# Where 16 output sums of a two-attention kernel are kept until they are stored

## The chip, the cores and the metric

The kernel runs on one core of one Trainium2 chip. The metric is device time in microseconds of one execution, lower is better; several executions give a median. A profile of one execution gives the time of each instruction on the core's engines: TensorE (PE, matrix products), VectorE (DVE), ScalarE (ACT), GpSimd (POOL) and SyncE (SP), and of the DMA transfers that SP, ACT and POOL issue. Each engine works through its own instructions in order and waits on semaphores where it needs another's result. In the profile's notation `ost<-g,r` is an instruction that reads the tiles g and r and writes ost.

## The reference, cut to what matters

Two attention layers on separate inputs, both of 2048 rows and 1024 columns with 32 heads, their outputs side by side:

```python
def _A_ref(x, wqkv, wo):      # each row looks at 8 rows, two apart
    qkv = (x @ wqkv) ...
    logits = einsum("bhsd,bhswd->bhsw", q, kg) * scale   # masked
    o = einsum("bhsw,bhswd->bhsd", softmax(logits), vg)
    return o @ wo
def _B_ref(x, wqkv, wo):      # each row looks at the 256 rows up to its own
    ...
    return o @ wo
return concatenate([_A_ref(...), _B_ref(...)], axis=-1)
```

All data is float32. The part that matters here is the last product of layer A, `o @ wo`.

## The kernel before

Work is cut into eight units of 512 rows: units 0 to 3 are layer B (dense), units 4 to 7 layer A (window). Each unit has eight groups of four heads; group s of unit u has the number hg = 8u + s, so the last is 63. A planner written in Python (`Clock`) simulates the engines with fixed durations and writes the instructions of all engines out in one order; what an engine does next is settled when the program is made, not while it runs. The semaphores between the engines are put in by the framework from what each instruction reads and writes.

A float32 product is made as three products of parts: `Stream.parts` splits a raw tile into a high part (a cast, L276 on ScalarE or L279 on VectorE) and a low part (the difference, L282 on VectorE), and each 128-row step of a product takes three matmuls (`mm`, L324, which is every matmul's line). Raw tiles are loaded by POOL's queue (L221) as tiles come free.

For layer A the outputs of two units are multiplied with `wo` together, in seven products instead of eight of half the size (`product(u, i)` for u = 4 and 6, i = 0 to 6). Products 0 and the like take tiles as they are; the others take sums of quarters, made earlier by VectorE (L1133) and kept in DRAM (`sd`, `td`), while the windows' outputs are kept in `od`. Each product has four column blocks n of four steps, so 12 matmuls per block; a block is summed in one of three PSUM banks ("g") and then added by VectorE (`add`, L902) to what the earlier products gave. These 14 products come at the end of the program, one after the other; the last steps of the last windows (groups 62 and 63: scores, mask L1214, softmax, values "o") lie between the first of them.

In products 1 and 4 an output block is complete. There are four blocks in each, so for two pairs of units 16 in all, counted by `where_o["ot"]`. Each is written by `add` to a tile o and stored from it by ScalarE's queue (L908). `going` holds stores that are not yet issued: a new sum first issues the older ones. Before the change, o was one of two things:

- the tile "ost" of the pool `stp`, which has a single buffer (`NST = 1`), so that each new sum there waits until the store of the one before has landed;
- columns 1024 to 1536 of `band[b]`, the working tile of the windows' softmax for even or odd groups, when group 62 + b is finished (`done["o"]`) and the count is not a multiple of three.

The seats are two stretches of the tile `pbuf`, one for even and one for odd groups, of 2 x 512 + 8 columns: the layer-A rows of queries (first 512) and keys (the rest) that the scores of a window read. In the profile they have the name pbuf. SP copies them there from the "nat" tiles (L608); `seat_free` notes in `done["scores"]` that the scores of a group have been issued. The last window's scores are those of hg = U * NG - 1 = 63.

Of the kernel before, what the change touches and what calls it, by code (L numbers as in the profile page):

```python
# [7 lines left out]
F32 = mybir.dt.float32  # L8
# [6 lines left out]
P = 128  # L15
NG = 8
NK = 8
S = 512
# [273 lines left out]
def kernel(ctx, tc, xs, wqk, wv, wo, outs, units):  # L292
# [3 lines left out]
    U = len(units)  # L296
# [10 lines left out]
    stp = ctx.enter_context(tc.tile_pool(name="stp", bufs=NST))  # L307
# [11 lines left out]
    def mm(out, left, right, **k):  # L319
        issued[0] += 4 if left.dtype == F32 else 2  # L320
        n = int(issued[0] + EXTRA - ASKED) // CHUNK
        if n > asked[0]:
            asked[:] = n, ck.now
        nc.tensor.matmul(out, left, right, **k)  # L324
# [30 lines left out]
    done = {}  # L355
# [102 lines left out]
    where_o = {"ot": 0, "s": 0, "bg": 0}  # L458

    def slot(i):  # L460
        return roomp.tile([P, 1024], F32, tag=f"r{i % NO}", name="r")
# [65 lines left out]
    seats = more[:, :2 * (2 * S + 8)].rearrange("p (b c) -> p b c", b=2)  # L527
    band, wide = [None, None], [None, None]
    halo = [[dram.tile([P, 2, 256], F32, name=f"halo{i}_{s}") for s in range(NG)] for i in range(2)]

    xt, xready, ot, rows, waiting = {}, {}, {}, {}, {}
# [32 lines left out]
    def latest(*ts):  # L564
        return None if any(t is None for t in ts) else max(ts)
# [288 lines left out]
    def product(u, i):  # L854

        out = []
        h = totals.setdefault(u, {})

        def ready(n, k):
            if n == 0 and k == 0:  # L860
                for j in range(2):
                    if ("s", u, i, j) not in held:
                        at = where["p", u, i, "s", j]
                        st.split_to(at + 1)
                        if at not in st.ready:
                            return None
                        held["s", u, i, j] = st.get(at)
            if n % 2 == 0 and k == 0 and ("t", u, i, n // 2) not in held:
                at = where["p", u, i, "t", n // 2]
                st.split_to(at + 1)  # L870
                if at not in st.ready:
                    return None
                held["t", u, i, n // 2] = st.get(at)
            x, r = held["s", u, i, k // 2]
            r = max(r[k % 2], held["t", u, i, n // 2][1])
            return latest(rg.when(), r) if k == 0 else r

        def run(n, k):
            if k == 0:
                h["ps"], h["b"] = rg.take()  # L880
            w, x = held["t", u, i, n // 2][0], held["s", u, i, k // 2][0][k % 2]
            c = S * (n % 2) + P * k
            for t, (a, b) in enumerate(TERMS):
                mm(h["ps"], w[:, a, c:c + P], x[:, b, :], start=(k == 0 and t == 0),
                                 stop=(k == 3 and t == 2))
            if k == 1:
                at = where["p", u, i, "t", 1]
                more_w = [kind for kind, _ in st.items[at + 1:at + 1 + (n + 1 if n else 0)]]
                while more_w.count("w") > 1 + n // 2:
                    more_w.pop()  # L890
                st.split_to(at + 1 + len(more_w))

        def after(n, k):
            if k < 3:
                return
            ps, bank = h["ps"], h["b"]
            if i == 0 and n % 2 == 0:
                h["ac", n // 2] = [slot(8 + 2 * g + n // 2) for g in range(2)]
            a, c = [t[:, S * (n % 2):S * (n % 2) + S] for t in h["ac", n // 2]]

            def add(dst, src):
                nc.vector.tensor_tensor(dst, ps, src, op=ALU.add)  # L902
                return ck.use("dve", 0.61, ck.now + ck.SEM)

            def store(r, col, tile, e):
                def go():
                    if going.pop(key, None):
                        nc.scalar.dma_start(outs[ORDER[u + r], 4 * col + n], tile)  # L908
                        ck.load("store", e)

                key = u, r, col, n
                going[key] = go
                ck.defer(e, go)

            if i in (1, 4):
                for f in list(going.values())[:-1]:
                    f()
                where_o["ot"] += 1
                b = where_o["ot"] % 2
                o = band[b][:, 1024:1536] if where_o["ot"] % 3 and U * NG - 2 + b in done["o"] else stp.tile([P, S], F32, tag="ost", name="ost")  # L920
            if i == 0:
                nc.scalar.copy(a, ps)
                e = ck.use("act", 0.485, ck.now + ck.SEM)
            elif i == 1:
                e = add(o, a)
                store(0, 0, o, e)
            elif i == 2:
                e = add(a, a)
            elif i == 3:
                e = add(c, a)  # L930
            elif i == 4:
                e = add(o, c)
                store(1, 0, o, e)
            elif i == 5:
                e = add(c, c)
                store(1, 1, c, e)
                e = add(a, a)
            else:
                e = add(a, a)
                store(0, 1, a, e)  # L940
            rg.give(bank, e)

        for n in range(4):
            for k in range(4):
                at = (n, k)
                out.append((lambda at=at: ready(*at), lambda at=at: run(*at), 3 * CG, lambda at=at: after(*at)))
        return out
# [611 lines left out]
    for u in range(U):  # L1559
        for s in range(NG):  # L1560
            a, b = attention(u, s)
# [58 lines left out]
    while True:  # L1620
# [21 lines left out]
        t, name = best  # L1642
# [54 lines left out]
```

## Time and profile before

| | |
|---|---|
| runs | 1792.06, 1794.24, 1795.07 us; median 1794.24 |
| the profiled execution | 1793.36 us |
| its span (first to last instruction) | 1791.7 us |
| mean granted clock of TensorE | 0.998 |
| busy: PE, VectorE, ScalarE, GpSimd | 1771.8, 1295.5, 936.3, 412.2 us |
| first and last sum at L902 | 1640.2 and 1787.6 us after the span's start |

Times in the profile's views are counted from the span's start. A row of a timeline has start, length, engine, line, operation, what is written and read, the count of merged instructions, and in brackets the engine's idle time just before with what ended it.

### The profile page before, as it was taken

What the parts mean: (1) busy time and instruction counts of PE and PEld (TensorE: products, weight loads), DVE (VectorE), ACT (ScalarE), POOL (GpSimd) and SP (SyncE); (2) the same over time, 40 slices, a digit from 0 to 9 for tenths busy, and PEclk for the clock granted to TensorE, in tenths of its full rate; (3) what the DMA queues carried; (4) which work ended last, traced back from release to release, by engine and by line L of the source; (5) the groups of instructions that cost most, each with busy time, mean ns of one, the idle gap of its engine ahead of it and who ended that gap; (6) DMA issues with size and microseconds to landing.
All of it is one profiled execution on the core that took longest, in us unless ns stands there. A gap on an engine that the chain in (4) does not pass through costs nothing.

```text
span 1791.7 us, 38433 instructions
## 1 busy us (share of the span) xinstructions
PE 1771.8 (99%) x14496; PEld 1443.6 (81%) x14496; DVE 1295.5 (72%) x2881; ACT 936.3 (52%) x2332; POOL 412.2 (23%) x962
## 2 busy tenths in 40 slices
PE   9999999999999999999999999999999999999999
PEld 7787777888778888878788788888888887887887
DVE  6777876768867769867678556566577869677966
ACT  5565566555656565656554524533354455455442
POOL 3322323222342223332223410100011101001210
PEclk9999999999999999999999999999999999999999
DMA  8355664644656556555556266666576769848984
GB/s 258 105 149 136 186 168 136 170 136 142 186 141 165 151 134 166 154 146 146 147 136 185 61 189 190 199 201 202 171 232 207 213 181 290 291 139 274 303 318 143
DMA packets 154793, 324.57 MB, mean 181 GB/s; under 512 B 18032, under 2 KB 58992, under 8 KB 154608
## 3 DMA queue, kind: packets, MB, share of 16 engines
q0 software_dynamic: 45792, 166.74, 30.9%
q1 hardware_dynamic: 98736, 137.02, 26.9%
q10 hardware_dynamic: 10080, 18.35, 2.8%
q8 instruction: 115, 1.88, 0.5%
q14 instruction: 70, 0.57, 0.1%
HBM read 201.33 MB, written 53.48 MB: 142 GB/s over the span
## 4 chain that ended last, share of the span: by engine, by line
PE 94%; DMA 2%; DVE 1%; ACT 1%; issue 1%; SPq 0%; DVEq 0%; ACTq 0%; POOLq 0%
PE g L324 74%; PE s L324 13%; PE o L324 7%; DMA outs<-ost 0%; DMA raw<-sd 0%; ACT s L1400 0%; DMA pbuf<-nat 0%; DVE w L282 0%; DMA raw<-wqk 0%; DMA raw<-xs 0%; DMA qst<-nat 0%; ACT w L276 0%; DVE r L1133 0%; DVE qst L1435 0%; DVE x L282 0%
## 5 line engine op out<-in xcount | busy, mean ns | idle before, releaser
L324 PE MATMUL g<-x,w 128*128 128x512 f32 x3552 | 879.1, 394 | 5.3 <-DVE ost L902 3.5
L324 PEld LDWEIGHTS g<-x,w 128*128 128x128 f32 x3552 | 658.6, 189 | 135.2 <-issue 10.7
L282 DVE TENSOR_TENSOR w<-raw,w 128x512 fp32r<-128x512 f32 x510 | 334.4, 697 | 53.7 <-ACT w L276 47.5
L1395 DVE CUSTOM_DVE_ANT_0 s<-s,mask_d 128x384 f32<-128x384 f32 (+2 forms) x512 | 261.8, 554 | 98.4 <-PE s L324 98.0
L1400 ACT ACTIVATE s<-s,nm 128x384 f32<-128x384 f32 (+2 forms) x512 | 274.4, 537 | 109.9 <-DVE nm L1395 103.3
L324 PE MATMUL g<-w,x 128*128 128x256 f32 (+1 forms) x1728 | 306.3, 327 | 0.5 <-DVE w L282 0.5
L1459 POOL TENSOR_SCALAR_AFFINE_SELECT pbuf<-pbuf 128x128 f32<-128x128 f32 (+1 forms) x605 | 219.8, 391 | 315.8 <-ACT pbuf L1480 313.8
L324 PEld LDWEIGHTS g<-w,x 128*128 128x128 f32 x1728 | 255.5, 190 | 25.2 <-DVE w L282 1.7
L324 PE MATMUL g<-r,w 128*128 128x512 f32 x960 | 238.5, 394 | 0.5 <-DVE r L1359 0.5
L1480 ACT ACTIVATE pbuf<-s 128x384 f32<-128x384 f32 (+2 forms) x480 | 203.4, 504 | 64.7 <-PE s L324 62.1
L324 PEld LDWEIGHTS g<-r,w 128*128 128x128 f32 x960 | 177.4, 188 | 36.0 <-DVE r L1359 1.1
L221 POOL DMA_DIRECT2D raw<-wqk x126 | 68.2, 541 | 389.2 <-DVE w L282 275.1
L324 PEld LDWEIGHTS s<-qst,kst 128*128 128x128 f32 x704 | 113.6, 189 | 42.0 <-ACT s L1400 16.8
L324 PE MATMUL s<-kst,qst 96*128 96x384 f32 (+2 forms) x512 | 142.3, 342 | 0.9 <-ACT s L1400 0.7
L324 PE MATMUL s<-qst,kst 128*128 128x256 f32 (+2 forms) x704 | 137.1, 302 | 4.0 <-ACT s L1400 3.2
L279 DVE CAST w<-raw 128x1024 fp32r<-128x1024 f32 x176 | 121.2, 689 | 8.6 <-PE g L324 7.8
L324 PEld LDWEIGHTS s<-kst,qst 96*128 96x128 f32 x512 | 93.6, 189 | 26.1 <-issue 4.5
L276 ACT CAST w<-raw 128x1024 fp32r<-128x1024 f32 (+1 forms) x80 | 82.4, 1037 | 47.9 <-PE g L324 15.9
L1400 ACT ACTIVATION_READ_ACCUMULATOR s<-s,nm 128x1 f32 x512 | 105.4, 206 | 0.0
L1260 ACT COPY wide<-band 32x512 f32<-32x512 f32 x128 | 79.0, 617 | 29.5 <-DVE band L1251 28.0
L324 PE MATMUL o<-pbuf,vbuf 128*32 128x384 f32 (+2 forms) x1408 | 91.1, 389 | 0.0
L625 ACT ACTIVATE nat<-g 128x512 fp32r<-128x512 f32 x64 | 38.3, 598 | 98.1 <-PE g L324 84.9
(91 smaller groups left out, 1428.1 us busy)
## 6 DMA issues: line engine op xcount, KB each, us to landing
raw<-wqk POOLq DMA_DIRECT2D x126, 512.0 KB, 4.7
raw<-wv POOLq DMA_DIRECT2D x60, 512.0 KB, 4.9
qst<-nat SPq DMA_DIRECT2D x96, 256.0 KB, 5.3
kst<-nat SPq DMA_DIRECT2D x96, 256.0 KB, 5.8
raw<-wo POOLq DMA_DIRECT2D x44, 512.0 KB, 4.5
raw<-xs POOLq DMA_DIRECT2D x28, 512.0 KB, 4.5
outs<-ost ACTq DMA_DIRECT2D x39, 256.0 KB, 3.1
kst<-halo SPq DMA_DIRECT2D x72, 128.0 KB, 4.5
```

What stands on the lines that cost most here:

```text
L221: (self.nc.scalar if early else self.nc.gpsimd).dma_start(raw if len(ap.shape) == 2 else raw.rearrange("p (a b) -> p a b", a=2), ap)
L276: nc.scalar.copy(t[:, 0, :], raw)
L279: nc.vector.tensor_copy(t[:, 0, :], raw)
L282: nc.vector.tensor_tensor(t[:, 1, c:c + 512], raw[:, c:c + 512], t[:, 0, c:c + 512].bitcast(F32), op=ALU.subtract)
L324: nc.tensor.matmul(out, left, right, **k)
L625: nc.scalar.activation(hl[:, 0, :], ps, AF.Copy, scale=sc)
L1260: nc.scalar.copy(diag[r:r + 32, :, :, c:c + 32], turned[r:r + 32, :, :, 1, :])
L1395: nc.vector.tensor_tensor_reduce(ps[:, :n], ps[:, :n], mask[:, cut:full], scale=-1.0, scalar=BIG, op0=ALU.add, op1=ALU.min, accum_out=nm)
L1400: nc.scalar.activation(ps[:, :n], ps[:, :n], AF.Exp, bias=nm, scale=-1.0, accum_out=sm)
L1459: nc.gpsimd.affine_select(w, w, pattern=[[0, m], [step, n]], compare_op=ALU.is_ge, fill=0.0, base=base, channel_multiplier=chan)
L1480: nc.scalar.activation(w, ps[:, :pack * n].rearrange("p (j n) -> p j n", j=pack), AF.Exp)
```

## The change

The choice of o for the 16 complete blocks is made in another way. Once the scores of the last window have been issued, o is one half (512 columns) of one of the two seats; the count chooses the seat by its parity and the half by the next bit. Until then it would be the pool tile. The bands are no longer used for sums.

```diff
             if i in (1, 4):
                 for f in list(going.values())[:-1]:
                     f()
                 where_o["ot"] += 1
-                b = where_o["ot"] % 2
-                o = band[b][:, 1024:1536] if where_o["ot"] % 3 and U * NG - 2 + b in done["o"] else stp.tile([P, S], F32, tag="ost", name="ost")
+                if U * NG - 1 in done["scores"]:
+                    b, at = where_o["ot"] % 2, where_o["ot"] // 2 % 2 * S
+                    o = seats[:, b, at:at + S]
+                else:
+                    o = stp.tile([P, S], F32, tag="ost", name="ost")
```

Here `seats` is `more[:, :2 * (2 * S + 8)].rearrange("p (b c) -> p b c", b=2)`, and `more` is all of `pbuf` as one row of columns.

## The prediction

> **What bounds the kernel now.** First the page's head and its chain of waits by engine:
>
> ```profile
> span 1791.7 us, 38433 instructions
> PE 94%; DMA 2%; DVE 1%; ACT 1%; issue 1%; SPq 0%; DVEq 0%; ACTq 0%; POOLq 0%
> ```
>
> PE sets the time nearly everywhere, so a changed wait is worth only what it takes out of PE's own sequence. Next the view of the line that makes the sums (L902): the forms written to the pool tile and to the bands, its semaphore instructions, and what VectorE sat idle for ahead of it:
>
> ```profile
> L902 DVE TENSOR_TENSOR ost<-g,r x7: 685/691/692, 1640.2 to 1763.1; 128x512 f32<-128x512 f32 x7
> L902 DVE TENSOR_TENSOR band<-g,r x9: 682/691/692, 1659.9 to 1766.9; 128x512 f32<-128x512 f32 x9
> L902 DVEq EVENT_SEMAPHORE  x36: 21/21/50, 1652.4 to 1784.9; - x36
>   DMA outs<-ost: 8.6, 2
>   DMA outs<-band: 1.9, 1
> ```
>
> Of 16 sums, 7 went to the pool tile and 9 to the bands; VectorE lost 8.6 us to the pool tile's stores and 1.9 us to a band's. How far PE feels this shows in the chain of waits in order of time (start, length, what):
>
> ```profile
> 1634.80 8.10 DMA raw<-sd
> ...
> 1642.92 1.14 ACT x L276 x2
> ...
> 1645.62 6.76 DMA outs<-ost
> ...
> 1660.01 0.61 DVE band L902
> ...
> 1677.80 109.76 PE g L324 x483
> ```
>
> and in PE's timeline:
>
> ```profile
> 1647.58 1.31 PE L324 MATMUL o<-wide,vbuf 128*32 128x8 f32 x40
> 1648.82 0.96 PE L324 MATMUL g<-x,w 128*128 128x512 f32 x3
> 1653.30 7.11 PE L324 MATMUL g<-x,w 128*128 128x512 f32 x24 [3.52 <-DVE ost L902]
> 1660.76 15.92 PE L324 MATMUL g<-x,w 128*128 128x512 f32 x69 [0.35 <-DVE band L902]
> ```
>
> There is one hole: ScalarE waited for a late load (landed 1642.90), so the first sum, added by 1640.90, was stored only from 1645.62 to 1652.38. The second sum needs the same tile, VectorE stood still, and PE had all three PSUM banks full. PE idles 3.52 and 0.35 us; afterwards it runs to the end, 0.2272 us a matmul (109.76/483). The 1.9 us before the last band sum are in no piece of this chain: PE does not feel them.
>
> **The change part by part.** VectorE and ScalarE around the hole:
>
> ```profile
> 1637.10 1.01 DVE L1214 TENSOR_TENSOR band<-s,near 128x160 f32<-128x160 f32 x4
> 1640.21 0.69 DVE L902 TENSOR_TENSOR ost<-g,r 128x512 f32<-128x512 f32 x1 [0.95 <-PE g L324]
> 1642.40 2.49 DVE L282 TENSOR_TENSOR x<-raw,x 128x512 fp32r<-128x512 f32 x4
> 1647.74 1.04 ACT L276 CAST w<-raw 128x1024 fp32r<-128x1024 f32 x1
> 1649.33 1.03 ACT L276 CAST w<-raw 128x1024 fp32r<-128x1024 f32 x1
> 1652.46 0.69 DVE L902 TENSOR_TENSOR ost<-g,r 128x512 f32<-128x512 f32 x1 [7.57 <-DMA outs<-ost]
> 1653.07 1.28 DVE L282 TENSOR_TENSOR w<-raw,w 128x512 fp32r<-128x512 f32 x2
> 1655.35 0.69 DVE L902 TENSOR_TENSOR ost<-g,r 128x512 f32<-128x512 f32 x1 [0.99 <-DMA outs<-ost]
> 1655.95 1.28 DVE L282 TENSOR_TENSOR w<-raw,w 128x512 fp32r<-128x512 f32 x2
> 1657.15 2.86 DVE L1133 TENSOR_TENSOR r<-r 128x512 f32<-128x512 f32 x4
> 1659.93 0.68 DVE L902 TENSOR_TENSOR band<-g,r 128x512 f32<-128x512 f32 x1
> ```
>
> *Which branch.* The mask of the last window (1637.10) stands ahead of the first sum (1640.21) in VectorE's order, and the code issues it after that window's scores. So the new condition holds at the first sum: all 16 sums go to the seats. Count 1 to 16 takes the halves in turn, each again after four; a group is four sums, so none waits for a store of its own group, and the previous group is tens of us back. Shapes, order and queues stay; no DMA is added or moved past another.
>
> *The chain of four sums.* (1) The second sum follows the four L282 that end at 1644.89: about 1644.95 to 1645.65. (2) VectorE's next stall is the first weight tile's low parts, which need ScalarE's cast, done at 1647.74 + 1.04 = 1648.78. I take 1648.83, against 1653.07: 4.24 us earlier. So 3.2 us of the 7.57 only change their name. (3) The third sum loses its 0.99 wait and follows 1.20 us later (the pitch 1655.95 to 1657.15): 1650.03, against 1655.35. (4) The second weight tile at 1650.63; its cast ends at 1650.36, in time. (5) From third to fourth sum VectorE took 4.58 us without a wait: 1654.61, ending 1655.29, against 1660.61.
>
> *What PE makes of it.* Before the hole PE ended at 1649.78. The next product's high parts are cast by 1648.78; its third matmul, at 1649.78 + 2 x 0.227 = 1650.24, is the first to need a low part, whose half is written by 1649.5. So PE goes straight on: 24 matmuls to 1655.23, then it needs the fourth sum's bank, 0.15 us behind its end as before (1660.61 to 1660.76): 1655.44. The gain is 1660.76 - 1655.44 = 5.32 us.
>
> The same from PE's side, with the granted clock by stretches (the numbers from PEclk on are clock, DMA share, GB/s):
>
> ```profile
> 1499.50:1502.90 3.40, 2.03 (x131) 1.71 (x120) 3.40 (x7) 2.20 (x5) 0.53 (x1) 0.96 0.75 209
> 1502.90:1506.30 3.40, 3.40 (x10) 2.71 (x9) 3.37 (x9) 1.04 (x1) 0.53 (x1) 0.54 1.04 352
> 1649.70:1653.10 3.40, 0.08 (x1) 0.00 (x0) 0.64 (x2) 0.66 (x1) 0.00 (x0) 0.96 0.15 58
> 1653.10:1656.50 3.40, 3.20 (x8) 2.63 (x9) 2.41 (x5) 0.64 (x2) 0.53 (x1) 0.54 0.51 169
> ```
>
> After the hole PE ran at about half clock for 3.4 us: 24 matmuls took 7.11 instead of 24 x 0.2272 = 5.45. So 3.52 + 0.35 + 1.66 = 5.53, less about 0.2 of new idle before the third block. The slow clock is not a separate gain: at full clock PE would have stood at the same bank until the fourth sum.
> The Trainium skill ("TensorE: Matmul & The Clock Gate", Part 1: The HAM clock gate) says that PE falls to half clock after an idle window of about 3.4 us and recovers after a busy one; the trace agrees in the second pair of rows. By that rule alone one would add the clock to the idle time, 5.5 us; by the order of the sums it is 5.3.
>
> *New waits.* The seat halves were last written by copies from the nat tiles and read by scores. The scores were over before their mask at 1637.10, but each first use may cost semaphore instructions: nothing to four of 0.050, so 0 to 0.2 us in front of the fourth sum. I take zero, as they would stand partly in VectorE's idle time, and keep both ends.
>
> *Does the rest shift as one block?* What follows hangs on VectorE and ScalarE, but loads already under way do not shift:
>
> ```profile
> 1643.98 0.53 POOL L221 DMA_DIRECT2D raw<-td  x1 [5.75 <-DVE x L282]
> raw<-td POOLq DMA_DIRECT2D x1, 512.0 KB, 7.0
> 1645.19 0.53 POOL L221 DMA_DIRECT2D raw<-td  x1 [0.68 <-DVE x L282]
> raw<-td POOLq DMA_DIRECT2D x1, 512.0 KB, 7.5
> 1661.10 1.05 ACT L276 CAST w<-raw 128x1024 fp32r<-128x1024 f32 x1 [2.47 <-DVE band L902]
> 1654.88 0.53 POOL L221 DMA_DIRECT2D raw<-od  x1 [9.16 <-DVE w L282]
> ```
>
> They land at 1650.98 and 1652.69; their casts move from 1661.10 to about 1655.8, so 3 us and more are left (the second cast is a us later). The next load (1654.88) is released by the first weight tile and moves only 4.24 us, into the tail of these two; the DMA share of 0.15 at 1649.7 to 1653.1 says that there is room. If contention still cost PE something, the two transfers overlap for at most 1652.69 - 1650.64 = 2.05 us; half of that, 1 us, is my bound. The stage after it ran 109.76 us without a gap and keeps its internal distances.
>
> Gain 5.3 us, bounds 3.6 (below) to 5.53. On the profiled execution's own time, 1793.36 (span 1791.7 and 1.66 around it): 1788.1. That execution lay 0.88 under the median of 1794.24; the forecast for a median is 1794.24 - 5.3 = **1788.9**.
>
> **The rivals.**
>
> *A. The hole closes, but a smaller wait keeps part of it.* A late load leaves 1 us (above); or the clock drops anyway. The row 1499.50 speaks for the latter: PE was busy 2.03 of 3.40 us, with small matmuls around 1.37 us of idle, and the clock was halved after it. In the changed kernel the 40 small matmuls of 1647.58 and any short wait at 1649.78 could fall in one such stretch. Price 3.4 x 0.5 = 1.7 us, gain 3.6: 1790.6. Against it: no wait is due there.
> The Trainium skill (same page, Why this matters for your kernels) advises no idle gaps over about 3 us; by it, this case could not occur, yet the row shows a drop after 1.37 us.
>
> *B. It does nothing.* If the seats belong to one tile whose parts are not kept apart, the second sum still waits for the first store: about 1794. Against it is how the windows used them:
>
> ```profile
> 1616.28 2.38 SPq L608 DMA_DIRECT2D pbuf<-nat  x4
> pbuf<-nat SPq DMA_DIRECT2D x2, 64.0 KB, 4.8
> 1619.57 1.47 PE L324 MATMUL s<-pbuf 32*32 32x40 f32 x128
> ```
>
> The last two copies into one seat, issued after 1618.0, landed after 1622.8; the scores of the other seat ran at 1619.57 to 1621.04 without waiting. Parts are kept apart there.
>
> *C. Slower.* One mechanism: the same lack of separation puts all 16 sums in single file, where before 9 had the bands. A single file cost 2.89 us from second to third sum and 12.25 from first to second, against a product column of 12 x 0.2272 = 2.73. Two spare banks cover 2 x 2.73 = 5.45. So three further groups stall from the point where a store takes over about 5.5 us more than the pace: 12.25 - 2.73 - 5.45 = 4.1 us. One such group beside the old hole gives 1794.24 + 4.1 = 1798.3; the row that speaks against B speaks against this too.
>
> **How the numbers follow.** Forecast 0.68 (1787.5 to 1790), A 0.17 (1789.9 to 1791.5), B 0.08, C 0.07. A difference under 0.2%, 3.6 us, can't be told from no change here: runs before spread over 1792.06 to 1795.07. The forecast's gain lies 1.7 us beyond that bound, A's lies on it. Faster: 0.62 from the forecast, 0.08 from A, 0.70 in all; slower 0.08 (C and a stray run); the same 0.22. The range goes from 1786.5 (5.53 and the runs' spread below their median, 2.2) to 1792.2 (A with 1.6 of spread); B and C lie outside, 0.15.
>
> **What would show it.** Right: 16 sums into pbuf at L902 and no idle time there for a store; the second sum at about 1645 and an idle stretch of some 3 us for the first weight cast after it; PE without a gap over 0.3 us between 1649 and 1656; full clock from 1650 on; the last sum at about 1782.3 instead of 1787.58. Wrong: a wait of L902 for "outs<-pbuf" (B, C), half clock after 1650 (A), or gaps in PE after 1656 that were not there before.

## The result, and the profile after

| | before | after |
|---|---|---|
| median of 12 runs | 1792.61 us (1791.20 to 1795.09) | 1788.90 us (1787.31 to 1791.04) |
| profiled execution | 1793.36 | 1788.09 |
| its span | 1791.7 | 1786.4 |

The ratio of the runs is 0.9979, with a 95% interval of 0.9971 to 0.9988: 0.21% faster, 3.7 us, between 2.1 and 5.2. The two profiled executions differ by 5.3 us.

The view of the summing line, after:

```profile
L902 DVEq EVENT_SEMAPHORE  x42: 21/21/4062, 1636.0 to 1779.5; - x42
...
L902 DVE TENSOR_TENSOR pbuf<-g,r x16: 681/691/692, 1640.3 to 1760.4; 128x512 f32<-128x512 f32 x16
its engine sat idle before it (us, times) until:
  PE g L324: 27.2, 22
  issue: 1.4, 1
```

All 16 sums go to pbuf, and VectorE no longer sits idle for a store: the two rows "DMA outs<-..." are gone. The timeline of VectorE and of ScalarE's queue around the old hole:

```profile
1644.86 0.68 DVE L902 TENSOR_TENSOR pbuf<-g,r 128x512 f32<-128x512 f32 x1
...
1645.73 0.34 ACTq L908 DMA_DIRECT2D outs<-pbuf  x1
...
1648.78 1.30 DVE L282 TENSOR_TENSOR w<-raw,w 128x512 fp32r<-128x512 f32 x2 [3.25 <-ACT w L276]
...
1650.00 0.68 DVE L902 TENSOR_TENSOR pbuf<-g,r 128x512 f32<-128x512 f32 x1
...
1650.60 1.28 DVE L282 TENSOR_TENSOR w<-raw,w 128x512 fp32r<-128x512 f32 x2
...
1654.58 0.68 DVE L902 TENSOR_TENSOR pbuf<-g,r 128x512 f32<-128x512 f32 x1
```

and of PE:

```profile
1647.57 1.29 PE L324 MATMUL o<-wide,vbuf 128*32 128x8 f32 x40
1648.79 6.44 PE L324 MATMUL g<-x,w 128*128 128x512 f32 x27
1655.40 15.90 PE L324 MATMUL g<-x,w 128*128 128x512 f32 x69 [0.18 <-DVE pbuf L902]
1671.24 1.18 PE L324 MATMUL o<-wide,vbuf 128*32 128x8 f32 x40
```

The first store is issued no earlier than before (1645.73, before 1645.62); the second sum simply does not wait for it. VectorE's idle time has another owner, 3.25 us for ScalarE's weight cast. PE has 0.18 us left of 3.87. The two profiles are a clean pair: the small matmuls of group 62 begin at 1647.58 and 1647.57. The granted clock (third number from the right) stays full:

```profile
1649.70:1653.10 3.40, 3.40 (x17) 2.78 (x16) 3.37 (x6) 3.12 (x6) 1.06 (x2) 1.00 0.86 291
1653.10:1656.50 3.40, 3.22 (x15) 2.38 (x14) 3.30 (x7) 0.93 (x2) 0.00 (x0) 1.00 0.92 325
```

### The profile page after: what moved, and what is told of

Its sections match the earlier page's. It is cut to its first block, busy times and chain, and to the rows that moved or that the text cites. A ratio compares the mean times of both kernels' runs of the same rounds, so it can differ in the third digit from the quotient of the medians.

```text
span 1786.4 us, 38443 instructions
## 1 busy us (share of the span) xinstructions
PE 1768.4 (99%) x14496; PEld 1440.2 (81%) x14496; DVE 1295.5 (73%) x2881; ACT 936.9 (52%) x2332; POOL 412.8 (23%) x962
## 4 chain that ended last, share of the span: by engine, by line
PE 92%; DVE 2%; DMA 2%; ACT 2%; issue 1%; SPq 0%; ACTq 0%; DVEq 0%; POOLq 0%
PE g L324 72%; PE s L324 13%; PE o L324 7%; DMA raw<-xs 1%; DVE w L282 1%; ACT s L1403 0%; DMA raw<-sd 0%; DMA pbuf<-nat 0%; DMA raw<-wqk 0%; DVE x L282 0%; ACT w L276 0%; DMA raw<-sx 0%; DMA qst<-nat 0%; ACT wide L1263 0%; ACT x L276 0%
```

## The experiments

Two questions are left by the result. Is the first group's chain the whole of it, as the prediction has it? And why do the profiles differ by 5.3 us and the medians by 3.7?

As a measure of the hole I use "the stretch" from the start of the small matmuls 'o' of group 62 to the start of those of group 63. The small matmuls of group 63 stand here in the timeline of the kernel before:

```profile
1676.61 1.18 PE L324 MATMUL o<-wide,vbuf 128*32 128x8 f32 x40
```

So the stretch took 1676.61 - 1647.58 = 29.03 us there, and 23.67 in the changed kernel. The expectations of the four runs with rings and with SP give it from the end of product 1's last block, 2.20 us less.

### Parts of the change

First group only:

```diff
-                b = where_o["ot"] % 2
-                o = band[b][:, 1024:1536] if where_o["ot"] % 3 and U * NG - 2 + b in done["o"] else stp.tile([P, S], F32, tag="ost", name="ost")
+                if where_o["ot"] <= 4:
+                    b, at = where_o["ot"] % 2, where_o["ot"] // 2 % 2 * S
+                    o = seats[:, b, at:at + S]
+                else:
+                    b = where_o["ot"] % 2
+                    o = band[b][:, 1024:1536] if where_o["ot"] % 3 and U * NG - 2 + b in done["o"] else stp.tile([P, S], F32, tag="ost", name="ost")
```

> Only the first four of the 16 sums go to the seats; the other 12 choose between the pool tile and the bands as before. Theory (all that PE gains is the hole in the first group): the same as the whole change, PE without a gap over 0.3 us from 1649 to 1656, and a median 3 to 4 us under the kernel before in the same rounds; in the last group VectorE again waits about 1.9 us for a store, and PE does not stop for it. Rival (the later sums bring a part as well): 1 to 2 us less gain than the whole change.

Measured: 1787.37 us, before in the same rounds 1792.33; ratio 0.9968 (0.9957 to 0.9980) over 6 runs. That is 5.0 us less, more than the 3 to 4 expected. PE's timeline and a row of the summing line's idle time:

```profile
1648.72 22.09 PE L324 MATMUL g<-x,w 128*128 128x512 f32 x96
```

```profile
  DMA outs<-band: 2.3, 1
```

96 matmuls without a gap, and VectorE's late wait for a band's store is back without costing PE anything. The other half, with `> 4` in place of `<= 4`:

> The counterpart: the first four sums choose as before, the other 12 go to the seats. Theory: no gain, within 1 us of the kernel before; the hole of the first group is there as before (PE idle 3 to 4 us), and the 1.9 us wait of VectorE in the last group is gone without PE being earlier for it. Rival (the later sums bring a part): 1 to 2 us faster.

Measured: 1792.38 against 1792.33, ratio 1.0000 (0.9991 to 1.0009). In its PE timeline the hole is there:

```profile
1653.55 7.16 PE L324 MATMUL g<-x,w 128*128 128x512 f32 x24 [2.62 <-DVE ost L902]
1661.01 15.89 PE L324 MATMUL g<-x,w 128*128 128x512 f32 x69 [0.30 <-DVE band L902]
```

PE idles 2.92 us here, close to the 3 to 4 expected. The four sums of the first group give the whole gain; the other 12 bring nothing that the runs show (the interval leaves 1.6 us either way). The intervals of the first group alone and of the whole change overlap, so that neither is shown to be the faster.

### How many halves it takes

The sums take n halves in turn (n = 1, 2, 3), always in the seats:

```diff
+                n_o = where_o["ot"] % n
+                b, at = n_o % 2, n_o // 2 * S
+                o = seats[:, b, at:at + S]
```

> The sums take two seat halves in turn instead of four. Theory (chain of sums): the second sum is free, the third waits for the first store, which is issued at 1645.6 in any case and lands at about 1652.4: third sum at 1652.4 instead of 1650.0, fourth 2.4 us later too. The stretch takes 21.5 + 2.4 = 23.9 us and the median lies halfway, 2 to 3 us under the kernel before. Rival (only the second sum's wait counts, since it is the one that PE's idle time is put down to): as good as four halves, 21.5 us.

Measured: 1790.06 against 1792.04, ratio 0.9987 (0.9979 to 0.9996); stretch 1673.99 - 1649.45 = 24.54.

```profile
1652.71 0.69 DVE L902 TENSOR_TENSOR pbuf<-g,r 128x512 f32<-128x512 f32 x1 [2.04 <-DMA outs<-pbuf]
...
1658.13 15.92 PE L324 MATMUL g<-x,w 128*128 128x512 f32 x69 [1.12 <-DVE pbuf L902]
```

The third sum waits for the first store, as the theory has it, and begins 3.26 us after the small matmuls of group 62; in the changed kernel it is 2.43. The stretch is longer by about the same, 0.87 instead of the expected 2.4, since PE came 1.9 us later in this execution (1649.45 against 1647.57). The rival (only the second sum counts) falls by the trace: the second sum waits for nothing, and PE still stops for 1.12 us at the fourth, where the changed kernel has 0.18. The times alone could not tell, because the interval overlaps that of the changed kernel.

> Three seat halves in turn. Theory: the fourth sum is the first that waits for a store, the first one, landed at about 1652.4, while VectorE comes to it at 1654.6: no wait that counts, the stretch takes 21.5 us as with four, time as the changed kernel (3.5 to 5 us under the kernel before). Rival (each store adds to the next one's delay, so that four are needed): between two and four halves, 22.5 to 23 us.

Measured: 1789.01, ratio 0.9983 (0.9974 to 0.9992), stretch 23.14. PE has no gap:

```profile
1648.18 22.09 PE L324 MATMUL g<-x,w 128*128 128x512 f32 x96
```

No sum waits for a store here, so in this profile three halves are enough; the rival would have the stretch at 24.7 to 25.2 us. The median is 3.0 us under the kernel before, less than the 3.5 to 5 expected, though the interval reaches to 4.7. With one half, a store can stand behind the next sum in the order of the program (`going` keeps the newest store back), so in this kernel some blocks of layer A's output hold the sum after theirs.

> All 16 sums in one and the same half of a seat: the single file of rival C. As a measure for the hole I take the stretch from the end of the last block of product 1 to the last group of small matmuls 'o', in which PE has 93 matmuls (21.1 us): the kernel before took 26.8, 27.8 in its second profile, the changed kernel 21.5. Theory (a wait costs PE only beyond the two spare PSUM banks, 5.45 us): first hole as before (26 to 28 us), the 12 later sums wait for stores on VectorE, some 1 to 4 us each, and PE stands still for less than 1 us over all three groups; time 0 to 1 us over the kernel before. Rival C as priced (one more group stalls by 4.1 us): 4 us slower.

Measured: 1793.78, ratio 1.0013 (1.0004 to 1.0022): slower. The timeline of VectorE, ScalarE and PE:

```profile
1644.81 0.68 DVE L902 TENSOR_TENSOR pbuf<-g,r 128x512 f32<-128x512 f32 x1
...
1645.53 0.34 ACTq L908 DMA_DIRECT2D outs<-pbuf  x1
...
1727.89 0.69 DVE L902 TENSOR_TENSOR pbuf<-g,r 128x512 f32<-128x512 f32 x1 [3.79 <-DMA outs<-pbuf]
...
1728.99 1.14 ACT L276 CAST x<-raw 128x512 fp32r<-128x512 f32 x2 [7.88 <-DVE pbuf L902]
...
1731.13 0.73 PE L324 MATMUL g<-x,w 128*128 128x512 f32 x2 [0.81 <-ACT w L276]
1733.34 54.24 PE L324 MATMUL g<-x,w 128*128 128x512 f32 x238 [1.47 <-DVE w L282]
```

The first hole is smaller than expected (stretch 26.22), because the second sum goes ahead of the first store. But from the 'o' of group 63 to the end it took 1791.7 - 1673.80 = 117.9 us, where the kernel before took 115.1. Neither expectation holds: the median is 1.7 us over the kernel before, and PE stands still for 2.3 us in the later groups. The later groups do cost something in single file, 2.8 us, less than rival C's 4.1, and not at the PSUM banks: VectorE waits for a store, ScalarE stands behind its own next store, whose sum VectorE has not made, and the casts of the next weights come late.

### Late issue or single tile

```diff
-                        nc.scalar.dma_start(outs[ORDER[u + r], 4 * col + n], tile)
+                        (nc.sync if (u, col, r) == (DU, 0, 0) else nc.scalar).dma_start(outs[ORDER[u + r], 4 * col + n], tile)
```

> The kernel before, with the four stores of the first group issued by SP instead of ScalarE; the tiles are as before. It asks how much of the hole is the late issue of the first store (added by 1640.9, issued at 1645.6 behind ScalarE's casts) and how much the single tile as such. Theory: the first store is issued at about 1641 and lands by 1648, before VectorE needs ScalarE's cast (1648.8); the third sum still waits for the second store, issued at about 1648.5 and 2 to 7 us under way. So the stretch shrinks to 22.5 to 25 us, half of the gain or more. Rival (the tile alone matters, whichever queue stores it): 26 to 28 us as before.

Measured: 1791.10 against 1792.04, ratio 0.9991 (0.9982 to 1.0000), stretch 26.36. SP's queue, ScalarE's cast of the late load, and VectorE:

```profile
1641.88 12.81 SPq L908 DMA_DIRECT2D outs<-ost  x3
...
1641.99 1.14 ACT L276 CAST x<-raw 128x512 fp32r<-128x512 f32 x2 [1.92 <-DMA raw<-sd]
...
1648.13 0.69 DVE L902 TENSOR_TENSOR ost<-g,r 128x512 f32<-128x512 f32 x1 [2.28 <-DMA outs<-ost]
...
1653.64 0.69 DVE L902 TENSOR_TENSOR ost<-g,r 128x512 f32<-128x512 f32 x1 [3.62 <-DMA outs<-ost]
```

The excess of the stretch over 23.67 is half of what it was (2.69 instead of 5.36), but this profile does not show that the early issue did it. The late load landed early as seen from PE: the 'o' of group 62 began at 1648.54, 6.6 us after the cast that waited for the load, where it was 4.7 us in the kernel before. With 6.1 us the kernel before took only 25.27 (its third profile, below). What the rows do show is that the place in ScalarE's queue is not all. The first store is issued 0.02 us after its sum has ended (1641.86), and still the second sum waits 2.28 us for it and the third 3.62 us for the second store. In the runs the early issue brings 0.9 us, less than the half of the gain that the theory expects, with an interval from no change to 3.2 us.

### The slow clock

14 matmuls fill the hole of the kernel before:

```diff
+            if (u, i, n, k) == (DU, 2, 0, 0):
+                warm = pss.tile([P, 512], F32, tag="s", name="s")
+                for _ in range(14):
+                    nc.tensor.matmul(warm, held["t", u, 1, 1][0][:, 0, :P], held["s", u, 1, 1][0][1][:, 0, :],
+                                     start=True, stop=True)
```

> The kernel before with 14 extra matmuls (128x128 weights, 512 columns, 14 x 0.227 = 3.2 us) into a PSUM bank that nothing reads, at the place where PE stops for the second sum. They fill the hole, so the granted clock should stay full, and nothing else is changed: the sums wait for the stores as before. Theory (the slow clock behind the hole is not a separate cost, because PE's third column block waits for the fourth sum in any case): clock 1.00 instead of 0.5 after the hole, PE reaches that bank 1.7 us earlier and waits 1.7 us longer for it, time as before within 0.5 us. Rival (idle time and slow clock add up): 1.7 us faster than the kernel before.

Measured: 1792.14 against 1792.33, ratio 0.9997 (0.9988 to 1.0006), stretch 29.18. PE's timeline, then the clock by stretches:

```profile
1648.23 3.37 PE L882 MATMUL s<-x,w 128*128 128x512 f32 x14
1652.12 5.85 PE L324 MATMUL g<-x,w 128*128 128x512 f32 x24 [0.52 <-DVE ost L907]
1659.58 15.89 PE L324 MATMUL g<-x,w 128*128 128x512 f32 x69 [1.60 <-DVE band L907]
```

```profile
1648.40:1651.80 3.40, 3.20 (x14) 2.28 (x13) 0.52 (x1) 0.58 (x1) 0.00 (x0) 1.00 0.22 89
1651.80:1655.20 3.40, 3.08 (x13) 2.39 (x14) 2.42 (x5) 0.59 (x1) 0.53 (x1) 1.00 0.48 164
```

The clock stays at 1.00, the 24 matmuls take 5.85 instead of 7.11 us, and PE gives it all back in front of the fourth sum: 1.60 us where it was 0.35. That is 1.25 us more, of the 1.7 expected.
The Trainium skill ("TensorE: Matmul & The Clock Gate", Part 1: The HAM clock gate) makes a window of idleness the cause of the half clock; that agrees, since filling the idle time alone removed it. The idle time need not fill the 3.4 us that the prediction quotes: in the run with the other groups alone the clock was 0.50 from 1653.5 to 1656.5, behind 2.62 us of idle time.

### Why the medians differ by less

> The kernel before, once more, unchanged. It asks why the median over runs moved by 3.7 us (1792.61 to 1788.90) when the two profiled executions differ by 5.3. Theory (the hole differs from execution to execution with the landing of the first sum's store, and the first profile showed a large one): here PE's idle time between 1640 and 1665 us is another one, 1.5 to 3 us instead of 3.9, and the store's landing shorter than 6.8 us. Rival (the hole is always the same, and the runs differ by something else, elsewhere in the program): again 3.5 to 4.0 us of idle time there, and fourth sum minus second sum as before; the lost 1.6 us must then be looked for at other places.

> The kernel before, unchanged, for a third profile. Theory: the later PE arrives after the small matmuls of group 62, the shorter the idle time at the second sum; the stretch from there to the 'o' of group 63 lies between 26 and 30 us (29.0 and 30.1 so far). Rival: always 29 to 30.

Measured: 1792.95 and 1791.69 us; ratios 1.0002 (0.9993 to 1.0010) and 1.0000 (0.9991 to 1.0009). The two profiled executions were the longest of the first set of runs, 1796.35, and the shortest of the other, 1788.51. First that of 1796.35, timeline and clock:

```profile
1644.93 1.14 ACT L276 CAST x<-raw 128x512 fp32r<-128x512 f32 x2 [3.89 <-DMA raw<-sd]
...
1647.63 0.34 ACTq L908 DMA_DIRECT2D outs<-ost  x1
...
1654.65 0.69 DVE L902 TENSOR_TENSOR ost<-g,r 128x512 f32<-128x512 f32 x1 [7.76 <-DMA outs<-ost]
...
1655.49 24.19 PE L324 MATMUL g<-x,w 128*128 128x512 f32 x93 [3.69 <-DVE ost L902]
```

```profile
1654.90:1658.30 3.40, 2.81 (x7) 2.26 (x8) 2.42 (x5) 0.59 (x1) 0.53 (x1) 0.50 0.41 154
1658.30:1661.70 3.40, 3.40 (x10) 2.64 (x9) 3.30 (x6) 2.18 (x4) 0.53 (x1) 0.52 0.90 237
```

then that of 1788.51:

```profile
1640.37 1.15 ACT L276 CAST x<-raw 128x512 fp32r<-128x512 f32 x2 [2.35 <-DMA raw<-sd]
...
1643.07 0.34 ACTq L908 DMA_DIRECT2D outs<-ost  x1
...
1647.60 6.62 PE L324 MATMUL g<-x,w 128*128 128x512 f32 x27
1647.61 0.69 DVE L902 TENSOR_TENSOR ost<-g,r 128x512 f32<-128x512 f32 x1 [3.81 <-DMA outs<-ost]
...
1655.90 15.93 PE L324 MATMUL g<-x,w 128*128 128x512 f32 x69 [1.69 <-DVE band L902]
```

From the cast of the late load to the issue of the first store it is 2.70 us each time. What differs is when the load lands, seen from PE (the 'o' of group 62 began 4.6 us after that cast in the longer one, 6.1 in the shorter one), and the store's way, 7.0 and 4.5 us. So the second sum begins 5.1 us after these matmuls in the one and 1.1 in the other; the stretches are 30.10 and 25.27. My first expectation, a smaller hole in the second profile, was wrong for that profile. It fits the rival, with 3.69 us of idle time and 7.46 us from second to fourth sum (7.47 before). The third profile speaks against the rival: its hole is all but closed at the second sum, and its stretch is below the range that I gave. There PE came earliest by the clock (1646.49, against 1649.51 in the longest), so its lateness counts only as seen from the load's landing.

The last pair makes PE late on purpose, by 9 matmuls ahead of product 1's second block:

```diff
+            if (u, i, n, k) == (DU, 1, 1, 0):
+                late = pss.tile([P, 512], F32, tag="s", name="s")
+                for _ in range(9):
+                    nc.tensor.matmul(late, held["t", u, 1, 0][0][:, 0, :P], held["s", u, 1, 0][0][0][:, 0, :],
+                                     start=True, stop=True)
```

> The kernel before, with 9 extra matmuls (9 x 0.227 = 2.0 us) into a PSUM bank that nothing reads, ahead of the second block of product 1, so that PE comes to the hole 2.0 us later while stores and sums stay where they are. It asks why the profiles differ by 5.3 us and the medians by 3.7. Theory (the hole ends when the first store has landed, so whatever makes PE late before it is absorbed by it): PE idles about 1.5 us instead of 3.5 at the second sum, the stretch from the last window's predecessor ('o' of group 62) to the 'o' of group 63 takes 2.0 us less than in the kernel before measured from PE's arrival, and the time is as before, 0 to 0.5 us over it. Rival (the two profiles were stray draws, lateness adds up in both kernels): 2 us slower than the kernel before.

Measured: 1792.47 against 1792.60, ratio 1.0001 (0.9992 to 1.0010), stretch 26.69.

```profile
1654.74 5.82 PE L324 MATMUL g<-x,w 128*128 128x512 f32 x24 [1.32 <-DVE ost L907]
1662.20 15.89 PE L324 MATMUL g<-x,w 128*128 128x512 f32 x69 [1.64 <-DVE band L907]
```

PE idles 1.32 us at the second sum (1.5 expected), and the stretch is 2.3 us shorter than 29.03 (2.0 expected). Two microseconds of extra work on PE cost nothing that the runs show (the interval reaches to 1.8 us over the kernel before): the hole takes them up.

> The same 9 extra matmuls in the changed kernel. Theory: there is no hole to absorb them (PE idled 0.18 us), so the time grows by 1.8 to 2.0 us over the changed kernel, and its lead over the kernel before shrinks to 2 to 3 us; with the kernel 'late before' the lead is smaller by the same 2 us. Rival: both grow by 2 us and the lead stays.

> The changed kernel, once more, unchanged, in the same rounds. Both theories: the same stretch takes 23.1 to 23.7 us, with no gap over 0.3 us in PE; median 3 to 5 us under the kernel before.

Measured: late 1790.07, ratio 0.9988 (0.9980 to 0.9997), stretch 23.13; unchanged 1789.13, ratio 0.9978 (0.9970 to 0.9987), stretch 23.69. The changed kernel loses 0.9 us by the extra work, half of what was expected, and its lead goes from 3.5 to 2.5 us; the two intervals overlap. The direction is the theory's, the size is not settled. Some 0.5 us can be taken up in the changed kernel too, since its stretch was 23.67 and the shortest on record, with PE never waiting, is 23.13.

## Why the prediction came out, point by point

- *Which branch.* As read from the order of VectorE's work: all 16 sums in pbuf.
- *The chain of four sums.* Predicted for the changed profile, and measured: second sum 1644.95 and 1644.86; first weight tile 1648.83 and 1648.78; third sum 1650.03 and 1650.00; second weight tile 1650.63 and 1650.60; fourth sum 1654.61 and 1654.58; PE's third block 1655.44 and 1655.40; last sum 1782.3 and 1782.2. The step that mattered was to follow VectorE on to its next wait, not to count its 7.57 us as gain.
- *The slow clock is no gain of its own.* Shown by the filled hole. It is not always so: in the second profile of the kernel before it lasted some 6.8 us, PE had no wait left at the fourth sum, and its 93 matmuls took 24.19 us instead of 21.13. There the slow clock, not the sum, set the end of the hole. By an estimate from this profile that cost some 0.8 us: the fourth sum ended at 1662.79, so PE could have begun the third block 0.15 us later, at 1662.94, and the 'o' of group 63 15.85 us after that, both as in the first profile: at 1678.79 instead of 1679.61.
- *New waits.* Six more semaphore instructions (42 against 36), the longest of them 4.06 us instead of 0.05; even so the first sum began 0.04 us later, the fourth 0.03 us earlier than forecast. Zero was the right end of the range.
- *The rest shifts as one block.* From the 'o' of group 63 to the end: 1786.4 - 1671.24 = 115.2 us, before 115.1.
- *Rival A.* No half clock after 1650 and no late load: it did not happen in the profile.
- *Rivals B and C.* Parts of a tile are kept apart, so both fell. C's mechanism exists, as the single half shows, but at another place and for 2.8 us.
- *The median: the term that was mis-sized.* "Gain 5.3 us" was worked out from one execution and carried over to the runs. They gave 3.7. That 1788.9 was met exactly is luck: the gain was 1.6 us too large, and the median of the three runs that it was taken from, 1794.24, lay as much above that of 12 runs, 1792.61. In place of the constant hole the runs showed one that changes: stretches of 29.03, 30.10, 28.29 and 25.27 us where the first four sums are as before (the kernel before three times, the other groups alone; mean 28.2), 23.67, 23.69, 23.13 and 23.14 where none of them waits for a store (the changed kernel twice, the first group alone, three halves; mean 23.4). A hole that ends with a store's landing also takes up lateness from before it. The mean difference of these profiles, 4.8 us, is still above 3.7, though inside the interval, and four profiles that lie between 25.27 and 30.10 cannot tell the two apart; whether absorbed lateness makes up that last microsecond is left open.

## What to carry to other kernels

To value a removed wait, follow the engine that waited to the next thing it needs, and stop at the engine that sets the end: here 7.57 us of idle time on VectorE were worth 5.3, and the 1.9 us later on nothing. A single buffer ties a sum to the landing of the store before it, and a store queued behind other work in order makes that late; three halves were enough where two left a wait. One profile gives the size of a hole in one execution; where a transfer's landing ends it, look at several before carrying its size over to a median.

## What was not expected of the hardware

Stores of the same 256 KB took 7.0 and 4.5 us from issue to the sum that waited for them, in two executions of one program. The half clock behind the same kind of idle time lasted 3.4 us in one execution and about 6.8 in another, where PE was already at work for 2.81 of the first 3.40 us. It came behind 2.62 us of idle time in one run, and not at all in the kernel before with 9 extra matmuls, where PE idled 1.32 and, 5.8 us later, 1.64 us.
